# A new order list for the operations of a retention, RWKV and Hyena kernel on one core

## The chip, the cores and the metric

The kernel runs on one core of one Trainium2 chip. The metric is the device time of one execution in microseconds. Engines are named as the profile names them: PE is the matrix engine (PEld its weight loads), DVE the vector engine, ACT the scalar engine, POOL the GpSimd engine, and SP the engine whose queue issues all transfers.

## The reference, cut to what matters

```python
# q, k, v: (2, 8, 768, 64); blocks of 64 tokens
intra = (qb @ kb^T * Dmask) @ vb          # Dmask: powers of lam, lower triangle
inter = (qb * lam_pow) @ kv_state
out_block = intra + inter
kv_state = lam**64 * kv_state + (kb * rev_pow)^T @ vb
# heads joined: x is (2, 768, 512)
xk = mu_k * x + (1 - mu_k) * x_prev;  xr = mu_r * x + (1 - mu_r) * x_prev
y = sigmoid(xr @ w_r) * (relu(xk @ w_k)**2 @ w_v)       # w_k: 512 x 1024, w_v: 1024 x 512
gate = sigmoid(conv5(y, conv_w))                         # five taps over the tokens
result = (gate * (y @ w_val)) @ w_out
```

All weights come as 64-bit floats; everything else is 32-bit.

## The kernel before, in words

**Stages.** There are 1536 tokens, in 12 chunks of 128 (attention), 6 groups of 256, and 3 pairs of groups of 512. A chunk `c` of attention makes transposed k and q, scores, masked scores, a state update and an output; chunks 0 to 3 are done whole, chunks 4 to 11 in halves of 64 tokens. Two groups of attention output give a pair `pr`, on which the layers then run: mix, receptance `r`, hidden `k`, value `v`, gate, val, projection. Each product is done in three passes with a high and a low part of both operands (lines 741 to 757), so an operand must first be split: `h` is a copy in the matrix format on ACT, `l` the remainder on DVE or POOL.

**Weights.** A weight piece is 128 rows of 512 64-bit numbers (512 KB). The function `conversion` (lines 310 to 352) makes 32-bit floats of it by steps named `a`, `b` (ACT, lines 328 and 330), `c`, `d`, `e` (DVE, lines 333 to 339), `f` (DVE or POOL, line 342), and then `h` (ACT, line 346) and `l` (DVE or POOL, line 348). Pieces `w0` to `w3` are w_r, `w4` to `w7` the first half of w_k, `w8` to `w11` its second half, `w12` to `w19` w_v, `y0` to `y3` w_val, `z0` to `z3` w_out.

**The order list.** Nothing is scheduled by the compiler: the string `ORDER` names all 1066 operations in one order, and every engine runs its own operations in that order. `name:E` puts an operation on engine E (V is DVE, G is POOL, A is ACT) where its definition allows more than one. An operation waits for what it reads and for the earlier users of its buffers. The names that matter here:

- `k0`, `q0`, `v0`, `w2`, `lam`, `mu` (a letter or word with one number): a load, issued by SP. The loads of k and q of chunks 0 to 5 are two issues each.
- `jq3.0` to `jq3.3`, `jk3.0` to `jk3.3`: the loads of q and k of group 3 (chunks 6 and 7), four issues of 32 KB each; `Bq3` and `Bk3` transpose them on DVE (line 461).
- `scan`: eight scans on DVE that make the decay mask (line 963); they read `lam` and `eye`. `quar`, `kd0`, `kd1`: copies of it on ACT. `pows`: nine small operations that make the powers `pw` (lines 981 to 998).
- `Tk0`, `Tq0`: four transposes on PE (line 440); `Ek0`, `Eq0`: their way out of PSUM; `Q1`: q times the powers; `D0`: k times its decay (line 480).
- `S0` scores, `M0` mask (lines 501 and 578, DVE), `U0` the state product, `O1` and `N1` the state update (lines 531, 534, 613, 616), `Y4` and `Z0` the output product, `X0` and `H0` its way out.
- `mr0.3.1a`, `b`, `h`, `l`: the mix for r of pair 0, block 3, group 1, and its split (lines 729, 734, 702, 704); `mk0.0a` and so on for k.
- `r0.10.0`: a unit of 12 matmuls of r (line 754); `k0.3.0`, `v0.2.0`, `a0.3.0`: units of 12 of the hidden, value and val products; `p1.0.0`: a unit of 6 wider ones of the projection (line 933).
- `k0.3e`, `h`, `q`, `l`: relu, square and split of the hidden product; `g0.1.2`: a tap of the gate (line 895); `s0.1h`, `l`: the split before val; `p1.0o`: a store.
- `warm3`: four matmuls on the identity without a use of their own.

**Buffers.** The ring `two` has 27 slots of 128x512, the ring `four` 6 of 128x1024, PSUM 4 slots of one bank. A slot is handed out at the first operation that names it, and that operation waits for the users of the slot before. Since SP is one queue, a load that waits for a slot holds all loads behind it.

**POOL and DVE.** In `emit`, every operation on POOL is made to wait for the DVE operation that stands last before it in the list:

```python
if o.engine == "G" and o.port and done is not None and last_v is not None:
    tc.add_manual_dep(done.ins, last_v.name, ..., reason="shared port")
```

Of the kernel before, what the change touches and what calls it, by code (L numbers as in the profile page):

```python
# [18 lines left out]


ORDER = """
    eye warm3 zero table w7 w7a w7c w7d w7e w4 lam w7b w4a w4c w4d w1 w4b w7f:V w4e w0 w1a q0
    Tq0 w4f:V w1c w1d pows k0 warm1 H0 w0a w0c w0d w0e Tk0 w0b k1 q1 warm2 Tk1 w7h Eq0:A k2 mu
    w1b w1e Ek0:A w7l:G w0f:G scan w1f:V S0 w4h w3 kd0 v0 D0:G Ek1:A Tk2 w1h Tq1 muT M0 w1l:V
    Eq1:A w3b w0h Q1 S1 w4l:V q2 D1:G U0 muc N0:A M1 v1 w3a D2:V Z0 X0:A Tq2 Eq2:A w6 Z1 Ek2:A
    w0l:V w3c O1:V Q2 w6a w3d X1:A H1:G q3 U1 w3e w6c mr0.3.0a:A mr0.3.0b mr0.1.0a:A mr0.1.0b
    v2 w6d mr0.0.0a:A mr0.3.0h mr0.3.0l:G S2 Tq3 N1 O2:G mr0.2.0a:A M2 mr0.0.0b k3 Tk3 Eq3:A
    Ek3:A mr0.1.0h w2 q4 Q3 k4 mr0.0.0h mr0.2.0b U2 quar kd1 S3 Z2 Tk4 w2a D3:G mr0.0.0l:G w2b
    M3 N2 X2:A w3f:V mr0.1.0l:V Tq4 v3 O3:V w2c w6b Ek4:A Z3 U3 Eq4:A w6e mr0.2.0h D4:V S4
    X3:A mr0.0.1a:A w2d v4 mr0.3.1a:A mr0.2.0l:G U4 k5 N3 q5 Q4 mr0.0.1b mr0.1.1a:A mr0.1.1b  # L30
# [9 lines left out]
    k0.1.1 w9l:V Q6:V w11h k0.0h w12c k0.3e:A w10e w11l:V k0.0q:A w12d jk5.0 Z5 w10f:V k0.1e:A  # L40
    k0.1h k0.1q:A k0.6.0 k6 D6:G w10h k0.4.0 k0.2e:A k0.2h X5:A M6 w13c w10l:V w16 k0.5.0
    k0.7.0 v10 jq5.2 U6 w13d k0.0l:V w16a N6.0:A w13e H3 w12e w15 w13f:V w15a w15c S7 w12f:V
    Q7:V k0.5.1 Y6 k0.3h O6.1:V w13h w12h w13l:V Z6 w14 N6.1 w15d w15b w12l:V k0.1l:V w14b
    O7.0:V w14a k0.7.1 k0.4.1 k0.7e:A k7 v0.3.0 D7:V X6:A w14c v7 w15e w17a k0.5e:A H2:G w17c
    w15f:G k0.4e:A jq5.1 U7 k0.6.1 N7.0 k0.2q:A k0.4h k0.5h M7 w15h w19 w14d w18 w18a w14e
    w16c w14f:V w17d jq5.3 Y7 w15l:V w16d w14h k0.6e:A k0.3q:A k0.4q:A v0.2.0 k0.2l:V w19a
    k0.3l:V v0.1.0 w14l:V k0.6h w17b w16b w17e k0.5q:A w16e v0.0.0 w17f:V v8 w19c w16f:V w17h
    Z7 w19d w17l:V k11 v0.1.1 w16h jq5.0 k0.7h k0.5l:V w16l:V v0.2.1 k0.4l:V w19e k0.6q:A
    v0.3.1 k0.7q:A k0.6l:V k0.7l:V w19b w19f:V v0.0.1 X7:A jq4.0 mk1.1a:A mk1.0a:A w18c
    mk1.3a:A w18b k9 w19h w18d w18e v0.3.2 w18f:V jk4.3 jq4.2 w18h O7.1:V v0.1.2 w19l:V w18l:V  # L50
    v9 v0.2.2 mk1.2a:A v0.0.2 mk1.1b mk1.1h mk1.0b jk4.1 k8 v0.0.3 mk1.1l:V v0.2.3 jq4.1
# [1033 lines left out]
```

## Time and profile before

| | us |
|---|---|
| median of 3 runs | 304.3 (303.47 to 306.48) |
| the profiled execution | 304.12 |
| its span, first to last instruction | 302.3 |
| PE, DVE, ACT, POOL busy | 279.1, 238.4, 162.6, 64.5 |
| mean granted clock of PE | 0.988 |

The profile shows one execution. Busy time of PE is modelled at the ends of its matmuls, so PE that shows as busy is not always PE at its full rate. L754 is line 754 of the kernel before; in the profile a buffer is named after the operation that first used it, without its first number (`b_mk_0h` is the high part of block 0 of a mix for k).

### The profile page before, as it was taken

The page shows a single profiled execution, that of the slowest core. Times are in us where ns is not written, and L with a number is a line of the kernel's source. Part 1 is how long each engine was busy: PE and PEld are TensorE (multiplying, and loading weights), DVE is VectorE, ACT ScalarE, POOL GpSimd, SP SyncE. Part 2 cuts the span into 40 slices and gives each one's busy share as a digit, 9 for nine tenths or more (in the row PEclk, how much of TensorE's full clock was granted, in tenths as well). Part 3 has the DMA queues.
Part 4 walks back from the last instruction along what each step waited for, and adds up shares of the span by engine and source line. Part 5 has one row for each costly group of instructions (what it writes and reads, how often), then busy time and mean ns, then how long its engine had stood idle before and what let it go on. Part 6 is the DMA issues. An engine that isn't in the chain of part 4 may idle for free.

```text
span 302.3 us, 7580 instructions
## 1 busy us (share of the span) xinstructions
PE 279.1 (92%) x3149; PEld 264.4 (87%) x3149; DVE 238.4 (79%) x397; ACT 162.6 (54%) x303; POOL 64.5 (21%) x69
## 2 busy tenths in 40 slices
PE   1469899869999999999999999999999999999995
...
GB/s 165 279 269 240 171 138 220 176 209 219 166 165 90 89 118 134 13 207 82 16 72 74 0 3 0 2 0 2 38 102 0 2 1 3 0 72 0 104 106 139
DMA packets 63489, 29.37 MB, mean 97 GB/s; under 512 B 58306, under 2 KB 58334, under 8 KB 63454
## 3 DMA queue, kind: packets, MB, share of 16 engines
...
q14 instruction: 10, 0.08, 0.1%
...
## 4 chain that ended last, share of the span: by engine, by line
PE 65%; DMA 12%; DVE 11%; SPq 4%; ACT 4%; issue 3%; DVEq 0%; ACTq 0%
PE b_k L754 16%; PE b_v L754 14%; PE b_p L933 11%; PE b_a L754 11%; PE b_r L754 7%; DMA xx<-in_moe_w_k_dram 5%; SPq L232 4%; DMA xx<-in_moe_w_r_dram 3%; PE xx L655 2%; DMA b_jk<-in_k_dram 2%; DMA b_w<-in_moe_w_v_dram 2%; DVE b_scan L963 1%; DVE w_v L348 1%; PE su L571 1%; DVE b_Bk L461 1%
## 5 line engine op out<-in xcount | busy, mean ns | idle before, releaser
L895 DVE SCALAR_TENSOR_TENSOR b_g<-xx,cw,b_g 128x512 f32<-128x512 f32 x48 | 38.7, 814 | 1.9 <-ACT b_g L897 1.1
L754 PE MATMUL b_k<-b_mk_0h,w_rk 128*128 128x256 f32 x96 | 24.8, 283 | 1.0 <-ACT xx L823 1.0
L754 PE MATMUL b_k<-b_mk_2h,w_rk 128*128 128x256 f32 x96 | 25.7, 291 | 0.0
L754 PE MATMUL b_k<-b_mk_3h,w_rk 128*128 128x256 f32 x96 | 24.5, 280 | 0.0
L754 PE MATMUL b_k<-b_mk_1h,w_rk 128*128 128x256 f32 x96 | 24.2, 277 | 0.0
L754 PE MATMUL b_r<-b_mr_0h,w_rk 128*128 128x256 f32 x96 | 20.1, 284 | 0.0
L754 PEld LDWEIGHTS b_k<-b_mk_0h,w_rk 128*128 128x128 f32 x96 | 18.0, 188 | 1.5 <-ACT xx L823 1.2
L754 PEld LDWEIGHTS b_k<-b_mk_2h,w_rk 128*128 128x128 f32 x96 | 18.6, 193 | 0.7 <-DVE w_rk L348 0.2
L754 PEld LDWEIGHTS b_k<-b_mk_3h,w_rk 128*128 128x128 f32 x96 | 18.4, 192 | 0.0
L754 PEld LDWEIGHTS b_k<-b_mk_1h,w_rk 128*128 128x128 f32 x96 | 18.1, 188 | 0.0
L754 PEld LDWEIGHTS b_r<-b_mr_0h,w_rk 128*128 128x128 f32 x96 | 15.9, 188 | 0.3
L754 PE MATMUL b_k<-b_mk_2l,w_rk 128*128 128x256 f32 x48 | 13.6, 283 | 0.0
L754 PE MATMUL b_k<-b_mk_3l,w_rk 128*128 128x256 f32 x48 | 13.4, 280 | 0.0
L754 PE MATMUL b_k<-b_mk_0l,w_rk 128*128 128x256 f32 x48 | 13.3, 277 | 0.0
L754 PE MATMUL b_k<-b_mk_1l,w_rk 128*128 128x256 f32 x48 | 13.3, 277 | 0.0
L754 PE MATMUL b_r<-b_mr_0l,w_rk 128*128 128x256 f32 x48 | 13.3, 277 | 0.0
L440 PE MATMUL b_Tq<-ident,b_q 128*128 128x128 f32 x24 | 4.8, 327 | 8.8 <-DMA b_q<-in_q_dram 8.8
L754 PE MATMUL b_v<-b_k_0h,w_v 128*128 128x256 f32 x48 | 12.3, 281 | 0.0
L754 PE MATMUL b_v<-b_k_2h,w_v 128*128 128x256 f32 x48 | 12.2, 279 | 0.0
L613 POOL TENSOR_TENSOR state<-state,pw 128x256 f32<-128x256 f32 x4 | 2.5, 622 | 45.4 <-DVE state L616 32.7
L754 PE MATMUL b_a<-b_s_3h,w_rk 128*128 128x256 f32 x48 | 12.1, 277 | 0.0
L754 PE MATMUL b_a<-b_s_2h,w_rk 128*128 128x256 f32 x48 | 12.1, 277 | 0.0
...
## 6 DMA issues: line engine op xcount, KB each, us to landing
...
```

The source lines that it names most:

```text
L232: e.dma_start(to, src)
L348: op(f"{key}l", "VG", lambda e: e.tensor_tensor(r(lo()), words(F32, 1), f32(hi()), op=ALU.subtract), reads=[raw, high, hi], writes=[lo])
L440: e.transpose(ps()[:, C * n:C * n + C], src()[:, C * n:C * n + C], ident)
L461: op(f"B{nm}{g}", "V", lambda e, raw=raw, t=t: e.transpose(t(), raw()), reads=[raw], writes=[t])
L571: e.matmul(su[half[j], s, Q * n:Q * n + Q], kt[half[s], n, t], qt[half[s], n, t], start=True, stop=True,)
L613: op(f"O{c}.{j}", "GV", lambda e, a=state_of[new], o=state_of[old]: e.tensor_tensor(a, o, pw[:, :, Q - 1:Q].to_broadcast([P, NPAIR, D]), o ...
L655: last = e.matmul(x[half[b_], j, at, :], w, m, start=spots[i] not in spots[:i], stop=spots[i] not in spots[i + 1:],)
L754: e.matmul(o, r(a), r(b), start=first and n == 0, stop=last and n == len(todo) - 1)
L895: e.scalar_tensor_tensor(t, src, w, t, op0=ALU.mult, op1=ALU.add)
L933: e.matmul(ps(), x, w, start=u == 0 and n == 0, stop=u == 1 and n == 5)
L963: e.tensor_tensor_scan(dmask_t()[:, s, n, :], lam_t()[:, h:h + 1].to_broadcast([P, C]), ident, 0.0, op0=ALU.mult, op1=ALU.add,)
```

## The change

The list `ORDER` is replaced by another one, with the same operations but for one (`warm7` takes the place of `warm1`), and `pows` may be put on DVE as well as on POOL. 103 of the 1066 operations change their engine: 33 go from DVE to POOL, 28 from POOL to DVE, 21 from DVE to ACT, 18 from ACT to DVE, 2 from POOL to ACT and 1 from ACT to POOL. No function is added. The part of the list up to `Bk3`, before and after, and the other line:

```diff
 ORDER = """
-    eye warm3 zero table w7 w7a w7c w7d w7e w4 lam w7b w4a w4c w4d w1 w4b w7f:V w4e w0 w1a q0
-    Tq0 w4f:V w1c w1d pows k0 warm1 H0 w0a w0c w0d w0e Tk0 w0b k1 q1 warm2 Tk1 w7h Eq0:A k2 mu
-    w1b w1e Ek0:A w7l:G w0f:G scan w1f:V S0 w4h w3 kd0 v0 D0:G Ek1:A Tk2 w1h Tq1 muT M0 w1l:V
-    Eq1:A w3b w0h Q1 S1 w4l:V q2 D1:G U0 muc N0:A M1 v1 w3a D2:V Z0 X0:A Tq2 Eq2:A w6 Z1 Ek2:A
-    w0l:V w3c O1:V Q2 w6a w3d X1:A H1:G q3 U1 w3e w6c mr0.3.0a:A mr0.3.0b mr0.1.0a:A mr0.1.0b
-    v2 w6d mr0.0.0a:A mr0.3.0h mr0.3.0l:G S2 Tq3 N1 O2:G mr0.2.0a:A M2 mr0.0.0b k3 Tk3 Eq3:A
-    Ek3:A mr0.1.0h w2 q4 Q3 k4 mr0.0.0h mr0.2.0b U2 quar kd1 S3 Z2 Tk4 w2a D3:G mr0.0.0l:G w2b
-    M3 N2 X2:A w3f:V mr0.1.0l:V Tq4 v3 O3:V w2c w6b Ek4:A Z3 U3 Eq4:A w6e mr0.2.0h D4:V S4
-    X3:A mr0.0.1a:A w2d v4 mr0.3.1a:A mr0.2.0l:G U4 k5 N3 q5 Q4 mr0.0.1b mr0.1.1a:A mr0.1.1b
-    O4.0:G M4 w2e w3h mk0.0a:A mr0.0.1h r0.01.0 Tk5 N4.0 w2f:V Tq5 w5 w5a w3l:V Eq5:A Ek5:A
-    mr0.1.1h jq3.0 v5 w5c w5b mr0.3.1b mr0.0.1l:V mr0.3.1h mr0.1.1l:V r0.00.0 S5 mk0.0b w5d
-    w2h w2l:V Y4 mr0.2.1a:A mr0.2.1b mr0.2.1h Z4 w6f:V r0.11.0 mk0.1a:A w5e mk0.1b mr0.3.1l:V
-    mr0.2.1l:V w5f:V jq3.2 mk0.3a:A mk0.2a:A w8 mk0.0h mk0.0l:V w9 mk0.2b w8a mk0.3b jq3.1
-    mk0.1h mk0.1l:V w11 w5h w5l:V O4.1:G jk3.0 jq3.3 M5 D5:G Bq3 jk3.1 r0.00.1 w11b w10
-    r0.10.0 w9a r0.00s r0.01.1 w8b r0.01s mk0.3h mk0.3l:V r0.11.1 r0.10.1 r0.11s k0.2.0 jk3.3
-    w9c k0.3.0 mk0.2h mk0.2l:V N4.1 r0.10s O5.0:V w6h w8c X4:A Q5 w10b w9d w9b k0.1.0 w6l:V
-    k0.0.0 w8d w11a w11c w9e k0.0.1 w13 k0.0e:A U5 w12 w9f:G jk3.2 w17 Bk3 w13b N5.0 w8e w11d
...
+    eye zero warm7 lam table scan w2 w2a k0 q0 quar Tk0 mu w2b w3 kd0 w3a w1 w2c w2d w2e w2f:V
+    Tq0 Eq0:A Ek0:V S0 D0:V H0 w2h warm2 k2 k1 w3b Tk1 w3c w1a w3d w3e w3f:V w3h kd1 w0 muT
+    w1b q1 pows:G muc w1c w0a w2l:V w1d Tk2 Ek1:A w3l:V w1e warm3 w1f:V v0 q3 D2:G Tq1 U0 M0
+    w1h Eq1:A N0:A Ek2:A w0c w1l:V S1 Tq3 w0d Q1 w0e q2 k3 D1:G M1 Eq3:A v1 w4 Tq2 Z0 Q3 Eq2:A
+    w0b Q2 X0:A S2 w0f:V O1:G Tk3 Ek3:A D3:G w4a U1 q4 w4b Z1 v2 w0h X1:A mr0.3.0a:A w5 M2 N1
+    O2:V mr0.1.0a:A S3 v3 w4c k4 mr0.2.0a:A U2 w4d w4e w0l:G mr0.0.0a:A Tq4 M3 N2 k5 mr0.2.0b
+    q5 mr0.1.0b Eq4:A w5a w4f:V Z2 X2:A mr0.0.0b w4h w5c mr0.3.0b w5d v4 O3:V mr0.3.0h
+    mr0.1.0h w7 w5e Q4 H1:G Z3 mr0.0.0h w4l:V Tk4 mr0.1.0l:V mr0.2.0h mr0.0.0l:V D4:G U3 Tk5
+    Ek4:A X3:A mr0.2.1a:A N3 S4 M4 Tq5 mr0.2.0l:V mr0.3.1a:A mk0.3a:A mr0.3.1b mr0.3.0l:V
+    mr0.1.1a:A mr0.0.1a:A mr0.0.1b mr0.1.1b Ek5:A O4.0:V Eq5:A r0.00.0 mr0.2.1b w6 mk0.1a:A v5
+    U4 N4.0 mk0.1b O4.1:V S5 w5b mr0.3.1h mk0.0a:A w7a w5f:V r0.01.0 D5:G M5 Y4 r0.01.1 mk0.1h
+    N4.1 mk0.0b mr0.2.1h mr0.1.1h mk0.2a:A mr0.3.1l:V cw0 w7c mr0.0.1h mk0.1l:V Z4 mk0.2b w6a
+    w8 mr0.0.1l:V mr0.1.1l:V mk0.0h mk0.3b w7d w8a r0.00.1 mr0.2.1l:V U5 w5h mk0.3h r0.10.0
+    w6c w10 w7b r0.10.1 w5l:V mk0.2h mk0.0l:V Q5 r0.11.0 r0.11.1 w7e r0.01s O5.0:V w6d r0.00s
+    mk0.2l:V w9 w7f:V r0.10s w6b w12 w6e mk0.3l:V w10b k6 k0.3.0 w6f:V w7h w7l:V w9a w12a w9c
+    w8c w11 w13 w12c w8b w9d w8d k0.2.0 r0.11s w11a w6h w6l:V w10a w10c w9e w11c w9b w13b
+    k0.1.0 jq3.3 w8e w13a jk3.1 N5.0 jq3.0 w13c w12b w11d w11b w9f:V jq3.2 jq3.1 k0.0.0 k0.0.1
+    X4:A w8f:V k0.1.1 w11e v6 w8h jk3.2 w10d w8l:V w9h w10e w9l:V w10f:V k0.3.1 k0.3e:A w12d
+    Y5 k0.1e:A Z5 w11f:V w13d w10h w12e w11h w11l:G Bq3 k0.2.1 k0.0e:A k0.3h k0.2e:A w10l:V
+    Q7:V jk3.3 k0.6.0 jk3.0 k0.4.0 w12f:V Q6:V D6:V k0.7.0 X5:A k0.2h w13e w13f:G k0.1h Bk3
...
-    op("pows", "G", powers, reads=[lam_b], writes=[pw_b])
+    op("pows", "GV", powers, reads=[lam_b], writes=[pw_b])
```


## Rows read from the trace of the kernel before

**Rows 1.** The page, parts 1 and 2: busy time; PE in forty slices of the span.

```profile
PE 279.1 (92%) x3149; PEld 264.4 (87%) x3149; DVE 238.4 (79%) x397; ACT 162.6 (54%) x303; POOL 64.5 (21%) x69
...
PE   1469899869999999999999999999999999999995
```

**Rows 2.** Windows: stretch, us, busy PE PEld DVE ACT POOL (instructions), PE clock, DMA, GB/s.

```profile
5.40:19.20 13.80, 6.55 (x45) 5.69 (x45) 12.75 (x24) 7.01 (x14) 6.91 (x12) 1.00 1.08 252
...
19.20:52.20 33.00, 30.19 (x505) 27.47 (x506) 31.99 (x60) 27.07 (x58) 7.54 (x9) 0.95 0.85 203
...
52.20:66.00 13.80, 10.16 (x94) 9.38 (x92) 9.13 (x18) 10.94 (x20) 2.93 (x3) 1.00 0.79 206
...
66.00:110.00 44.00, 43.06 (x600) 41.39 (x601) 40.70 (x77) 32.58 (x58) 2.65 (x4) 0.96 0.60 142
...
150.00:233.00 83.00, 82.92 (x811) 82.47 (x810) 71.12 (x111) 39.27 (x74) 25.65 (x19) 1.00 0.09 27
```

**Rows 3.** The chain that ended last, in order of time: start, us, what.

```profile
178.62 21.76 PE b_k L754 x192
...
254.79 11.01 PE b_p L933 x48
```

**Rows 4.** Timeline of the start, all engines: start, us, engine, line, operation, [idle before].

```profile
1.63 0.42 SPq L953 DMA_DIRECT2D b_lam<-in_lam_dram  x1
...
4.73 0.66 ACT L328 ACTIVATE b_w7a<-b_w 128x512 f32<-128x512 f32 x1 [2.51 <-DMA b_w<-in_moe_w_k_dram]
...
8.06 0.87 POOL L988 COPY pw<-b_lam 64x4 f32<-64x4 f32 x2 [6.29 <-DMA b_lam<-in_lam_dram]
...
11.34 1.29 PE L440 MATMUL b_Tq<-ident,b_q 128*128 128x128 f32 x4 [8.76 <-DMA b_q<-in_q_dram]
...
13.95 4.74 DVE L963 TENSOR_TENSOR_SCAN b_scan<-b_lam,ident 128x128 f32<-128x128 f32 x8
...
20.69 1.16 PE L494 MATMUL su<-b_Eq,b_Ek 64*128 64x128 f32 x16 [2.81 <-ACT b_Eq L443]
```

**Rows 5.** Timeline of DVE (first five) and PE from 51 to 107 us.

```profile
51.56 0.68 DVE L348 TENSOR_TENSOR w_rk<-xx,w_rk 128x512 fp32r<-128x512 f32 x1
...
53.92 1.25 DVE L461 STREAM_TRANSPOSE b_Bq<-b_jq 128x1024 f32<-128x1024 f32 x1 [1.08 <-DMA b_jq<-in_q_dram]
...
60.99 0.43 DVE L333 TENSOR_SCALAR b_w11a<-b_w11a 128x512 f32<-128x512 f32 x1 [0.94 <-ACT b_w11a L328]
...
64.46 1.25 DVE L461 STREAM_TRANSPOSE b_Bk<-b_jk 128x1024 f32<-128x1024 f32 x1 [2.45 <-DMA b_jk<-in_k_dram]
...
104.91 1.29 DVE L348 TENSOR_TENSOR w_v<-b_w,w_v 128x512 fp32r<-128x512 f32 x2
...
53.80 0.39 PE L754 MATMUL b_k<-b_mk_0h,w_rk 128*128 128x256 f32 x1 [1.00 <-ACT xx L823]
...
106.45 0.28 PE L754 MATMUL b_v<-b_k_6h,w_v 128*128 128x256 f32 x1
```

**Rows 6.** Groups of DVE instructions from 5 to 110 us: busy us, mean ns, idle before.

```profile
L348 DVE TENSOR_TENSOR w_rk<-xx,w_rk 128x512 fp32r<-128x512 f32 x8 | 5.5, 692 | 0.0
...
L704 DVE TENSOR_TENSOR b_mr_0l<-b_mr_0a,b_mr_0h 128x256 fp32r<-128x256 f32 x5 | 1.9, 416 | 0.0
```

**Rows 7.** Timeline of the SP queue: loads of the transposed blocks, four issues each.

```profile
37.92 4.93 SPq L232 DMA_DIRECT2D b_jq<-in_q_dram  x4
...
43.88 2.09 SPq L232 DMA_DIRECT2D b_jq<-in_q_dram  x4
...
50.19 2.16 SPq L232 DMA_DIRECT2D b_jq<-in_q_dram  x4
```

**Rows 8.** Timeline of DVE and of POOL beside each other, late in the span.

```profile
206.29 0.75 DVE L895 SCALAR_TENSOR_TENSOR b_g<-xx,cw,b_g 128x512 f32<-128x512 f32 x1
...
208.63 3.24 DVE L895 SCALAR_TENSOR_TENSOR b_g<-xx,cw,b_g 128x512 f32<-128x512 f32 x3
...
208.88 1.65 POOL L882 TENSOR_TENSOR b_s_3l<-xx,b_s_3h 128x512 fp32r<-128x512 f32 x1 [5.39 <-DVE b_z2a L339]
```

More of the change, by code (lines that the diff above doesn't have):

```diff
@@ L40 @@
[L40 to L51, printed above, removed]
@@ new lines @@
+    O7.0:G M7 Z6 w13h w13l:V w15c w14 k7 k0.6e:A v7 v0.2.0 k0.2q:A w14a k0.2l:V w15b w14c w17a
+    w15d v0.1.0 D7:V w15e w14d U7 k0.7e:A v0.3.0 w15f:V k0.5h w17c k0.5q:A w14e w14b X6:A w15h
+    N7.0 Y7 Z7 w14f:V w16 w14h w16a w15l:V w17d w14l:V jq4.0 w19 k0.7h w16c w17e w17b w18 w16d
+    H3 w17f:V w16e w19a w19c jq4.2 w16b v0.0.0 jk4.2 w16f:V w17h H2:G w18a w17l:V v0.0.1 x0
+    w16h w18c v0.3.1 k0.5l:V w16l:V X7:A k0.4l:V k0.6h w19b w18b w19d w18d w19e k9 w18e w19f:V
+    v9 w18f:V k0.6q:A v0.2.1 mk1.1a:A jq5.1 jk4.0 mk1.3a:A mk1.0a:A k0.6l:V w19h k0.7q:A
@@ new lines @@
+    w19l:V mk1.2a:A v0.1.1 v0.2.2 k0.7l:V w18h w18l:V k8 v0.3.2 mk1.3b jq4.1 v0.1.2 mk1.3h
+    mk1.0b v0.0.2 mk1.1b v0.2.3 mk1.0h mk1.1h mk1.0l:V v0.3.3 v0.3e mr1.3a:A v0.1.3 mk1.2b
+    mk1.1l:V v0.0.3 jq4.3 jk4.1 O7.1:G v0.2e v0.1e k1.1.0 k1.2.0 cw mk1.3l:G N7.1 D9:G v8
+    jk4.3 k1.5.0 Bq4 jq5.3 cwa v0.0e D8:V k1.7.0 mk1.2h jq5.2 mk1.2l:V Q8:V k1.5.1 Bk4 U8 S8
+    x1.1:A k1.2.1 O8.0:G N8.0 M8 Y8 mr1.0a:A k1.1.1 k10 D10:V cwc O8.1:V mr1.2a:A k1.5e:V v10
+    Z8 k1.1e:A N8.1 S9 cwb cwd cwe cwf:G cwg U9 X8:V mr1.0b O9.0:V y2 k1.1h k1.4.0 k1.4.1
@@ new lines @@
+    r1.3.0 k1.7h k1.4l:G k1.0q:A r1.1.1 r1.1s r1.3.1 k1.6h k1.0l:V k1.2q:V k1.2l:V M11 z3a y2d
+    z3c y2e x1.0:A k1.6q:V v1.3.0 x2.3:A k1.7q:A Z11 g0.0.0:A g0.1.2 v1.1.0 r1.0s v1.1.1
+    v1.2.0 v1.2.1 z3d y3b H5:G z3e k1.5h k1.5q:G k1.6l:V y3a x3 z1a X11:A y1 mk2.0a:A z1c
+    k1.5l:G z3f:V mr2.2a:A mk2.2a:V r1.3s mk2.3a:A x2.2:A v1.0.0 mk2.3b v1.2.2 mk2.1a:A y0
+    mk2.1b k1.7l:V mr2.2b mk2.0b mk2.0h y0a mk2.0l:V mk2.1h g0.1.3 z1b v1.3.1 v1.3.2 v1.3.3
+    v1.3e v1.0.1 v1.0.2 y3c y3d y3e y3f:G y1a y1c v1.1.2 y1d v1.1.3 mk2.1l:G v1.0.3 v1.0e
```

81 lines of the change are left out of this document (36 added, 45 removed).

## The prediction

> **What bounds the kernel now.** I read the page first, then the windows, then the chain. PE is busy for 92% of the span, and its forty slices show where it isn't: the first quarter [rows 1]. The windows say who holds it there. From 5.4 to 52.2 us DVE is busy for 12.75 of 13.8 us and 31.99 of 33.0; from 66 to 110 us for 40.70 of 44; while PE has 82.92 of 83 us between 150 and 233 [rows 2]. The later part of the chain is units of PE alone: 16 units of 12 matmuls in 21.76 us, 1.36 us each, and 48 projection matmuls in 11.01 us [rows 3]. So until about 106 us PE gets its operands just as DVE finishes them, and from there on PE runs through.
>
> The hinge is piece `w18`. Its low part is the second of two DVE instructions that end at 104.91 + 1.29 = 106.20 us, and the first value unit that reads it starts at 106.45 [rows 5]. Both lists place the same PE work ahead of that unit: 37 units of r, hidden and value (37 x 1.36 = 50.3 us) and the same transposes, attention products and warm-ups (by PE's groups 29.2 us), 79.5 us in all; so PE is 27 us late there. The same work follows it in both. Hence the end moves as the end of `w18l` on DVE moves, as long as nothing behind it binds.
>
> I count DVE as *work* (each listed operation by its group's mean, less 0.08 us by which neighbours overlap) and *lag* (time minus work). Before, the list up to `w18l` has 160 DVE operations, 87.3 us of work: the lag is 106.2 - 87.3 = 18.9 us. Its parts: 5.4 until DVE starts, since the first piece arrives for ACT at 4.73 [rows 4]; 2.2 more by the end of mask `M0` at 20.4; 2.2 more by the end of `w5l` at 52.24 (42.4 us of work, lag 9.8); 4.5 of waits for late transfers, namely 1.08 for `jq3`, 0.94 for `w11` by way of ACT, 2.45 for `jk3` [rows 5]; 0.6 more by 66 us; and 4.0 from there to 106, of which 2.8 are waits for PE and for ACT behind it. The idle time in the windows is 5.4 + 1.05 + 1.0 + 4.7 + 3.3 = 15.4 [rows 2]; the other 3.5 is instructions that took longer than their mean.
>
> **The change part by part.**
>
> *Amount of work.* Total arithmetic stays. Up to `w18l` the new list has 164 DVE operations, 89.2 us: +1.9. It gives DVE three more half splits (3 x 0.34) and two more `f` steps (2 x 0.61), one `l` step less (-0.61) and two small shifts around the copies of k (+0.3); prices are 692 and 416 ns less the overlap [rows 6]. Over the whole list DVE falls from 217.3 to 215.2, so behind `w18l` it has less than before. ACT rises by 1.7 of 151 and POOL by 3.5 of 63; neither is near full in any stretch [rows 2].
>
> *The start.* Before, `lam` is issued at 1.63, behind two weight pieces, and read at 8.06; the eight scans start at 13.95, after three pieces' work, and the first q arrives at 11.34 [rows 4]. In the new list `lam` is the first issue (at 0.74) and `scan` the first DVE work. The trace shows no `lam` load alone. From below: the last `jq3` load is issued until 52.35 [rows 7] and read at 53.92 [rows 5], 1.6 us later, so 0.74 + 0.42 + 1.6 = 2.8; from above: its own 8.06 - 1.63 = 6.4 us, 7.1. A full 512 KB piece takes 4.0 (0.74 to 4.73), and `lam` is a few KB, so I take 2.9, and scan from 3.3 to 8.0. The masks' copies on ACT then hold `w2b` and so `w2f`, which I put at 0.7 of DVE idle. Lag 4.0 after the start in place of 7.6 at `M0` (3.6 saved), up to 8.2 if `lam` takes its 6.4 (nothing saved). With q0 and k0 as third and fourth large loads, at 250 KB per us [rows 2], q0 is there at about 7 us and not at 11.3; `M0` ends at 13.9 us of work + 4.0 = 17.9, and v0, due at 17, is in time.
>
> *The powers.* `pows` may go to DVE, but the new list keeps it on POOL, later (behind `w3f`). The nine operations take 4.8 us there, from 8.06 on [rows 4]; `Q1` needs them at 18.9 and they end about 18.1. Cost 0, with 1.6 if POOL is held up; gain 0.
>
> *The middle.* Between 20 and 52 us both lists feed DVE with the same kinds of operations, and loads are as dense: I keep the 2.2 lost there before (bounds 0 and 4.4). At 39.4 us of work the r unit `r0.10.0` gets its last split: 39.4 + 4.0 + 2.2 = 45.6, with 29.7 of PE work ahead of it; the first hidden unit comes 5.4 later, at 51.0, against 53.80 [rows 5].
>
> *The j loads.* `Bq3` comes at 60.8 us of DVE work and `Bk3` at 65.6, where `w5l` plus little stood before: at lag 6.2 they are due at 67.0 and 71.8. SP is one queue. In it `k6` waits for a slot of the ring `two` that block 0's split gives back at about 48.6, and `w11`, `w13`, `v6` and eight j loads stand behind it: 48.6 + 1.8 for the single loads + 8 x 2.09 [rows 7] = 67.1, landed 2 later at 69.1. `Bk3` starts near 70.6, so 1.4 hides it, and the three waits of 4.5 us in all go. Without that cover, see the rival.
>
> *To `w18l`.* Of 4.0 lost before from 66 on I keep 2.3: PE's waits shrink as the list puts fewer of DVE's inputs right behind PE (bounds 1.2 and 4.0). Sum: lag 4.0 + 2.2 + 2.3 = 8.5; `w18l` ends at 89.2 + 8.5 = 97.7, which is 8.5 before 106.2. DVE's lag falls by 10.4, and 1.9 goes back as added work.
>
> *Behind it.* PE has 189.5 us of work left and took 298.7 - 106.4 = 192.3; I keep these 2.8 (among them the half-clock stretches that pull the mean to 0.96 [rows 2]), and the 3.6 us from the last matmul to the span's end and 1.8 outside it. The profiled execution took 304.12, 0.2 under the median of 304.3, so the two stand for each other: 304.1 - 8.5 = 295.6.
>
> **The rivals.**
>
> *DVE loses nothing after the start (B).* Lag 4.0 at `w18l`: 93.2, 13.0 earlier, 291.1 us. For it: the list is made from these durations, and 31.99 of 33.0 shows that DVE can be fed. Against: even there 2.2 were lost, and PE would have to be as regular.
>
> *POOL beside DVE (C).* A POOL operation of 1.65 us ran beside three taps on DVE, and these took 3.24 us for 3 x 0.75 = 2.25: 0.99 lost [rows 8]. Eleven POOL operations of 0.6 to 1.4 us stand before `w18l` in the new list; at 0.99 each they cost 10.9 in place of the 4.5 that I keep: 304.1 - 8.5 + 6.4 = 302.0. Against it: before, 13 such operations stood there, and all lengthening was 3.5, under 0.3 each.
> [...]
>
> *The SP queue (D, slower).* Eight j loads stand close behind `k6`. One took 4.93 us where others took 2.09 [rows 7]. If all go at 4.93, they end at 50.4 + 39.4 = 89.8, landed 91.8; `Bk3` ends at 93.1, and the 23.6 us of DVE work from there give `w18l` at 116.7: 304.1 + 10.5 = 314.6. It decides from 3.6 us per load on (then `w18l` is back at 106.2); a slot for `k6` that comes 12 us later does the same. Against: of the loads before, one alone was that slow, and they went at 2 us beside more traffic.
>
> *The list gives nothing where it binds (E).* `pows` doesn't move to DVE; if `lam` lands late and the middle loses 4.4, the lag is 14.9 and the time 302.0: no change that can be told.
>
> **How the numbers follow.** Forecast 0.50, B 0.13, C 0.18, D 0.10, E 0.09. What a measurement here can tell from no change is 1%, 3.0 us: faster is below 301.3. The forecast and B lie there whole, and of C and E, centred just above it, somewhat over half; that makes 0.79 faster. 0.12 is the rest of C and E and D's mild end; 0.09 slower is D. The forecast's own range is 290.5 to 300 (`lam` late: +4.2; the middle: 2.2 either way). The range from B's foot to C's upper side, 289.5 to 303.5, leaves D and the edges out.
>
> **What would show it right or wrong.** Right: scan before 4 us; the first q transposes near 7; DVE busy in all of 5 to 100 us; first hidden unit near 51; no wait for `jq` or `jk` in front of the transposes on DVE; `w18l` near 98; PE without gaps behind it, last matmul near 290. Wrong: idle time before `Bk3` that ends with a DMA (D); DVE splits over 1 us beside POOL (C); scan not before 7 (E); or gaps of PE after 110 us, since then the step "nothing behind it binds" fails.

## The result, and the profile after

| | before | after |
|---|---|---|
| median, us | 304.39 (4 runs) | 294.75 (294.27 to 295.52, 4 runs) |
| ratio to before, 95% interval | | 0.9649 (0.9611 to 0.9686) |
| the profiled execution, us | 304.12 | 294.27 |
| its span, us | 302.3 | 292.5 |
| last matmul ends, us | 298.72 | 288.87 |
| PE, DVE, ACT, POOL busy, us | 279.1, 238.4, 162.6, 64.5 | 278.7, 231.2, 163.7, 75.6 |
| mean granted clock of PE | 0.988 | 1.000 |

The forecast was 295.6 us. The page of the new kernel, parts 1 and 2 (busy time; PE and its clock in forty slices), against [rows 1]:

```profile
PE 278.7 (95%) x3149; PEld 262.6 (90%) x3149; DVE 231.2 (79%) x389; ACT 163.7 (56%) x307; POOL 75.6 (26%) x73
...
PE   3799989999999999999999999999999999999995
...
PEclk9999999999999999999999999999999999999999
```

PE's busy time is the same to 0.4 us; what went is its idle time in the first quarter. The same stretches as in [rows 2], with the same columns:

```profile
5.40:19.20 13.80, 11.17 (x80) 8.95 (x81) 12.86 (x24) 10.48 (x23) 6.03 (x11) 1.00 1.25 274
19.20:52.20 33.00, 30.55 (x503) 26.94 (x502) 32.82 (x66) 28.57 (x56) 7.70 (x8) 1.00 0.84 230
52.20:66.00 13.80, 13.69 (x174) 13.36 (x173) 12.01 (x26) 11.55 (x22) 1.31 (x1) 1.00 0.53 99
66.00:110.00 44.00, 43.55 (x585) 42.03 (x586) 40.54 (x69) 30.94 (x55) 13.89 (x10) 1.00 0.66 155
...
150.00:233.00 83.00, 83.00 (x734) 83.00 (x734) 68.94 (x101) 39.28 (x76) 22.25 (x16) 1.00 0.04 14
```

Read the column of matmuls: from 5.4 to 19.2 us PE is busy for 11.17 us where it was 6.55, and from 52.2 to 66 for 13.69 where it was 10.16. DVE, third of the busy columns, is busy for 32.82 of 33.0 in the second stretch. The clock is 1.00 throughout, where it was 0.95 and 0.96. The timeline of the start, against [rows 4]:

```profile
0.74 0.36 SPq L953 DMA_DIRECT2D b_lam<-in_lam_dram  x1
...
3.70 2.63 DVE L963 TENSOR_TENSOR_SCAN b_scan<-b_lam,ident 128x128 f32<-128x128 f32 x8 [3.70 <-DMA b_lam<-in_lam_dram]
...
7.34 1.21 PE L440 MATMUL b_Tq<-ident,b_q 128*128 128x128 f32 x4
...
10.33 2.08 PE L494 MATMUL su<-b_Eq,b_Ek 64*128 64x128 f32 x16 [1.78 <-ACT b_Eq L443]
```

`lam` is there at 3.70, the first q transposes run at 7.34 and not at 11.34, the first scores at 10.33 and not at 15.54, as the row of before below has it (the row of [rows 4] at 20.69 is `S1`). The eight scans take 2.63 us where they took 4.74.

```profile
15.54 1.16 PE L494 MATMUL su<-b_Eq,b_Ek 64*128 64x128 f32 x16
```

The timeline of DVE around the j loads and at the end of `w18l`, against [rows 5]:

```profile
65.53 1.25 DVE L461 STREAM_TRANSPOSE b_Bq<-b_jq 128x1024 f32<-128x1024 f32 x1 [1.33 <-issue]
...
70.90 1.25 DVE L461 STREAM_TRANSPOSE b_Bk<-b_jk 128x1024 f32<-128x1024 f32 x1 [0.55 <-DMA b_jk<-in_k_dram]
...
95.86 0.69 DVE L348 TENSOR_TENSOR w_v<-b_w,w_v 128x512 fp32r<-128x512 f32 x1
```

and the SP queue in front of them, against [rows 7]: `k6`, which waited for its slot, then the j loads.

```profile
47.25 0.38 SPq L232 DMA_DIRECT2D b_k<-in_k_dram  x1
...
48.78 1.91 SPq L232 DMA_DIRECT2D b_jq<-in_q_dram  x4
50.73 4.69 SPq L232 DMA_DIRECT2D b_jk<-in_k_dram  x4
...
55.46 6.14 SPq L232 DMA_DIRECT2D b_jq<-in_q_dram  x12
...
62.15 7.36 SPq L232 DMA_DIRECT2D b_jk<-in_k_dram  x12
```

The last j load is issued until 69.51 (67.1 was worked out), one of the eight loads at 4.69 us and the others at 1.9 to 2.5. `Bk3` starts at 70.90 (70.6) and waits 0.55 us instead of 2.45: the cover was 0.5 us too thin, no more. In front of `Bq3` the page names no cause; the last of `jq3`'s issues, at 61.16, took 4.1 us to land (median of those beside it 2.0), so this 1.33 too was most likely a load's. `w18l` ends at 95.86 + 0.69 = 96.55, 9.65 earlier than the 106.20 of [rows 5]; the last matmul comes 9.85 earlier.

### The profile page after: what moved, and what is told of

Same layout as the page of the kernel before. It is cut to its first block, busy times and chain, and to the rows that moved or that the text cites. A ratio compares the mean times of both kernels' runs of the same rounds, so it can differ in the third digit from the quotient of the medians.

```text
span 292.5 us, 7610 instructions
## 1 busy us (share of the span) xinstructions
PE 278.7 (95%) x3149; PEld 262.6 (90%) x3149; DVE 231.2 (79%) x389; ACT 163.7 (56%) x307; POOL 75.6 (26%) x73
## 4 chain that ended last, share of the span: by engine, by line
PE 84%; DVE 5%; ACT 4%; SPq 2%; DMA 2%; issue 1%; DVEq 0%; ACTq 0%
PE b_v L754 23%; PE b_k L754 19%; PE b_p L933 11%; PE b_r L754 11%; PE b_a L754 11%; PE xx L655 3%; SPq L232 2%; PE xx L553 2%; DMA xx<-in_moe_w_v_dram 1%; PE su L571 1%; PE su L592 1%; DMA b_lam<-in_lam_dram 1%; DVE b_scan L963 1%; DVE b_M L501 1%; PE su L494 1%
## 5 line engine op out<-in xcount | busy, mean ns | idle before, releaser
L895 DVE SCALAR_TENSOR_TENSOR b_g<-xx,cw,b_g 128x512 f32<-128x512 f32 x48 | 44.7, 952 | 0.5
L754 PE MATMUL b_k<-b_mk_2h,w_rk 128*128 128x256 f32 x96 | 24.9, 283 | 0.0
L754 PEld LDWEIGHTS b_k<-b_mk_2h,w_rk 128*128 128x128 f32 x96 | 18.0, 188 | 0.4
L903 ACT ACTIVATE b_g<-b_g 128x512 f32<-128x512 f32 x12 | 7.3, 628 | 15.6 <-DVE b_g L895 15.6
L870 DVE TENSOR_TENSOR xx<-b_v,xx 128x512 f32<-128x512 f32 x12 | 8.1, 683 | 6.9 <-PE b_v L754 6.8
L754 PE MATMUL b_v<-b_k_1h,w_v 128*128 128x256 f32 x48 | 12.2, 279 | 0.2 <-ACT b_k_7e L847 0.2
L754 PE MATMUL b_a<-b_s_1h,w_rk 128*128 128x256 f32 x48 | 12.1, 276 | 0.0
```

Source lines behind the costliest of these rows:

```text
L754: e.matmul(o, r(a), r(b), start=first and n == 0, stop=last and n == len(todo) - 1)
L870: op(f"v{pr}.{rb}e", "V", lambda e: e.tensor_tensor(x2_at(pr, rb), two(ps), x2_at(pr, rb), op=ALU.mult), reads=[ps], writes=[x2_b[pr, rb]])
L895: e.scalar_tensor_tensor(t, src, w, t, op0=ALU.mult, op1=ALU.add)
L903: op(f"g{pr}.{n}s", "A", lambda e: e.activation(acc(), acc(), AF.Sigmoid), writes=[acc])
```

## Where the time went

DVE's account up to `w18l`, from the traces of the two kernels. An instruction's time counts from the end of the one before it, and what it takes beyond its group's mean is lengthening. The scans turned out to take 2.63 us when nothing holds them; they count 2.63 in the work of both:

| us up to the end of `w18l` | before | after |
|---|---|---|
| DVE starts | 5.4 | 3.7 |
| idle afterwards | 10.0 | 4.1 |
| instructions longer than their mean | 5.6 | 1.6 |
| work | 85.2 | 87.1 |
| end | 106.2 | 96.5 |

So 1.7 us came from the start, 5.9 from waits, 4.0 from instructions that no longer grow, and 1.9 went into more work. Of the 4.0 some 3.3 stand in instructions that overlap one on POOL. This is DVE's account, not a price list: some of its parts, put alone into the old list, gain nothing, as the experiments show.

PE's account says what reached the end. Busy time up to the first unit that reads `w18`, before and after, with the columns of [rows 2]:

```profile
0.00:106.45 106.45, 87.63 (x1214) 81.31 (x1214) 91.07 (x168) 78.16 (x148) 21.20 (x35) 0.97 0.76 185
...
0.00:97.38 97.38, 87.56 (x1214) 79.71 (x1214) 89.56 (x173) 78.47 (x148) 26.54 (x33) 1.00 0.80 197
```

The same 1214 matmuls take the same 87.6 us; PE's idle time falls from 18.8 to 9.8 us. Of these 9.0 us, 3.3 fall before 20 us, 1.5 between 20 and 38, and 4.2 behind. From 39 us on PE waits in the new list for nothing longer than 0.23 us.

## The experiments

Line numbers of the experiments' kernels are 5 lower than those above, since the list takes fewer lines. First the parts of the gain, put one by one into the list of before.

**The start alone.**

```diff
-    eye warm3 zero table w7 w7a w7c w7d w7e w4 lam w7b
+    eye warm3 zero table lam scan w7 w7a w7c w7d w7e w4 w7b
...
-    w1b w1e Ek0:A w7l:G w0f:G scan w1f:V
+    w1b w1e Ek0:A w7l:G w0f:G w1f:V
```

> The list of before, with lam issued first and the scans first on DVE; nothing else moves. Theory (the gain is a sum of DVE's lag saved at the start and of waits for transfers taken away later): DVE is about 4 us earlier until 50 us, but Bq3 and Bk3 still wait for loads that SP issues at its own pace, so most of it goes into a longer wait in front of Bk3 (2.45 us before, 4 to 6 now): 302.5 to 304.4. Rival (the start alone explains nearly half of the change): 300.0 to 300.8, with Bk3's wait near 2.5.

Measured: 304.62 us, ratio 0.9976 (0.9937 to 1.0016). The timeline of DVE, where it waits:

```profile
3.46 2.85 DVE L958 TENSOR_TENSOR_SCAN b_scan<-b_lam,ident 128x128 f32<-128x128 f32 x8 [3.46 <-DMA b_lam<-in_lam_dram]
...
17.28 1.22 DVE L496 TENSOR_TENSOR b_M<-su,b_scan 128x1024 f32<-128x1024 f32 x1 [2.22 <-PE su L489]
...
63.28 1.25 DVE L456 STREAM_TRANSPOSE b_Bk<-b_jk 128x1024 f32<-128x1024 f32 x1 [3.56 <-DMA b_v<-in_v_dram]
```

The scans are done 12 us earlier, but the mask needs scores, and these need q, which still lands at 11.4: 2.22 us are lost there. `Bk3` takes another 3.56. `w18l` ends at 105.98, 0.2 earlier than before. An early `lam` alone is worth nothing in the old list. The rival falls; the theory holds in its direction only: DVE is 1.9 us earlier at the first mask (18.50, not 20.41), not 4, the wait in front of `Bk3` is under its 4 to 6, and the time lies 0.2 above its range.

**One transpose out of the way.** `Bk3` behind five other DVE operations, and its reader `S6` two units later:

```diff
-    U5 w12 w9f:G jk3.2 w17 Bk3 w13b N5.0 w8e w11d
-    w8f:V w11e w13a w12a k0.2.1 w10a w10c Y5 S6 w9h k0.3.1
+    U5 w12 w9f:G jk3.2 w17 w13b N5.0 w8e w11d
+    w8f:V w11e Bk3 w13a w12a k0.2.1 w10a w10c Y5 w9h k0.3.1
...
-    w11f:V w12b k0.1.1 w9l:V
+    w11f:V w12b k0.1.1 S6 w9l:V
```

> The list of before, with Bk3 moved five DVE operations later (behind w11e) and S6, which reads it, two units later on PE. Theory: DVE works through its 2.45 us wait for jk3, PE's 3.0 us wait for the state in front of S6 goes: DVE 2.0 to 2.5 earlier from there on, 301.8 to 302.5. Rival (the wait is hidden anyway, since the next splits wait for something else): 303.8 to 304.6.

Measured: 301.27 us, ratio 0.9888 (0.9841 to 0.9934). In DVE's timeline the wait is gone:

```profile
64.55 1.25 DVE L456 STREAM_TRANSPOSE b_Bk<-b_jk 128x1024 f32<-128x1024 f32 x1
```

`w18l` ends at 103.12, 3.1 earlier, and the time is 3.5 us under the runs beside it: more than the 2.45 of the wait and a little more than the theory gave. Two more waits of the kernel before are gone here, PE's in front of `Y5`, for the state that `N5.0` makes behind `Bk3`, and a later one of DVE for PE:

```profile
66.16 0.69 PE L655 MATMUL xx<-b_Q,state 64*64 64x64 f32 x16 [2.78 <-DVE state L616]
...
88.31 0.42 DVE L616 TENSOR_TENSOR state<-su,state 128x256 f32<-128x256 f32 x1 [1.23 <-PE su L592]
```

In this execution the wait for `jq3` is 0.9 us shorter too, which the edit doesn't explain, and DVE's instructions are 1.7 us longer, so the parts are not to be taken to the tenth. Two names moved give a third of the whole gain.

**Both.**

> Both edits together on the list of before. Theory: more than the sum, since the early start is no longer lost in front of Bk3: 4 to 6 us, 298.5 to 300.5. Rival (each is hidden by something else in turn): 302 or more.

Measured: 301.21 us, ratio 0.9890 (0.9843 to 0.9936): no more than with `Bk3` alone. The theory falls; the time lies 0.8 under the rival's 302, but its mechanism, that something else hides the early start, is what the timelines show. PE's and DVE's:

```profile
28.45 0.84 PE L435 MATMUL b_Tk<-ident,b_k 128*128 128x128 f32 x4 [2.21 <-DMA b_k<-in_k_dram]
```

```profile
32.06 1.23 DVE L496 TENSOR_TENSOR b_M<-su,b_scan 128x1024 f32<-128x1024 f32 x1 [1.71 <-PE su L489]
```

The old list asks for `k3` so late that PE waits 2.21 us for it, and the mask `M3` on DVE 1.71 for PE. In the new list the loads of k and q follow the scans forward, so the lead is kept, as the next run shows.

**The start taken out of the new list.** `lam` third:

```diff
-    eye zero warm7 lam table scan w2 w2a k0 q0 quar
+    eye zero warm7 table w2 w2a k0 lam scan q0 quar
```

> The new list with lam issued third, behind w2 and k0, as it stood behind two pieces before. Theory: the scans start at about 8 instead of 3.70, DVE has nothing else in front of them, and its lag is 3.5 to 4.5 larger up to w18l: 298.2 to 299.3. Rival (the start is absorbed by slack later): 294.5 to 295.3.

Measured: 296.61 us, ratio to before 0.9739 (0.9692 to 0.9787). `lam` lands 2.6 us later and not 4:

```profile
6.33 2.63 DVE L958 TENSOR_TENSOR_SCAN b_scan<-b_lam,ident 128x128 f32<-128x128 f32 x8 [6.33 <-DMA b_lam<-in_lam_dram]
```

`w18l` ends 2.1 later and the time is 1.9 longer. Both expectations are missed, the theory's by its size: I had put the landing at 8. What is lost at the start passes on to the end nearly one for one, which in the old list it did not.

**A wait of ACT.** On top of the `Bk3` run, `N6.0` behind `w15a` on ACT:

```diff
-    k0.0l:V w16a N6.0:A w13e
+    k0.0l:V w16a w13e
...
-    w13f:V w15a w15c
+    w13f:V w15a N6.0:A w15c
```

> The list of before with Bk3 and S6 later, as in the run that came to 301.27, and with N6.0 on ACT moved behind w15a, so that ACT's wait for PE no longer stands in front of w15. Theory (what DVE lost between 66 and 106 us were waits for other engines at the heads of queues): the 1.59 us wait of w15c on DVE goes, 299.5 to 300.2. Rival (another wait takes its place before w18): 301.0 to 301.5.

Measured: 305.58 us, ratio 1.0019 (0.9975 to 1.0062): both fall. ACT's timeline in the run that it builds on:

```profile
75.30 0.38 ACT L605 ACTIVATE state<-su 128x256 f32<-128x256 f32 x1
77.56 0.67 ACT L323 ACTIVATE b_w15a<-xx 128x512 f32<-128x512 f32 x1 [1.88 <-DMA xx<-in_moe_w_v_dram]
```

and ACT's and PE's in this one:

```profile
78.50 0.66 ACT L323 ACTIVATE b_w15a<-xx 128x512 f32<-128x512 f32 x1 [2.56 <-DMA xx<-in_moe_w_v_dram]
```

```profile
79.48 0.69 PE L566 MATMUL su<-b_Bq,b_Bk 64*64 64x64 f32 x32 [2.91 <-ACT state L605]
```

In the `Bk3` run `w15a` was held by its own load, not by `N6.0`, which was done 1.9 us before. The premise came from the profile of before, where ACT does run the two back to back, behind a wait of 2.24 us for PE. With `N6.0` moved behind `w15a`, the state update came late for PE. In this execution another 2.62 us of DVE went in front of `Bq3` at 54.53, ahead of the edit, so how much of the 4.3 us to the `Bk3` run the edit cost stays open. A wait that is named after an engine can be a transfer's that this engine waits for, as here the 1.88 us of `w15a`'s load, and it is to be read in the profile of the list that is edited.

**Powers beside the scans, and powers on DVE.** Two runs of the new list, `pows` directly behind `lam`, and `pows:V` at its place:

```diff
-    eye zero warm7 lam table scan w2
+    eye zero warm7 lam pows:G table scan w2
...
-    w1b q1 pows:G muc w1c
+    w1b q1 muc w1c
```

```diff
-    w1b q1 pows:G muc w1c
+    w1b q1 pows:V muc w1c
```

> The new list with pows put directly behind lam, so that POOL makes the powers while DVE runs the eight scans. Theory (a POOL operation beside a DVE operation with two operands lengthens it): the scans take 4.4 to 4.9 us instead of 2.63, DVE is 1 to 2 us later at the first mask, of which the stretch of the old place of pows gives back up to 1: 295.0 to 296.3. Rival (the scans were long before for another reason): scans 2.6 to 2.9, 294.0 to 294.9.

> The new list with the nine operations of pows on DVE at the same place, which the other line of the change permits. Theory: 9 operations of 0.1 to 0.2 us on the engine that is full there, 1 to 1.8 us, less the 0.5 to 1 us by which POOL's powers lengthened DVE between 10 and 16 us: 294.9 to 296.0. [...]

The first took 294.91 us (0.9660, 0.9635 to 0.9685), no different from the new list, and the theory's mechanism fails for operations as small as these: with the powers beside them the scans took 2.85 us, 0.22 more than in the new list:

```profile
3.75 2.85 DVE L958 TENSOR_TENSOR_SCAN b_scan<-b_lam,ident 128x128 f32<-128x128 f32 x8 [3.75 <-DMA b_lam<-in_lam_dram]
```

The second took 296.60 us (0.9719, 0.9687 to 0.9750), 1.85 more than the new list and a little beyond what the theory gave. The nine operations on DVE:

```profile
12.54 0.34 DVE L983 COPY pw<-b_lam 64x4 f32<-64x4 f32 x2
12.92 1.85 DVE L989 TENSOR_TENSOR pw<-pw 128x4 f32<-128x4 f32 x7
```

They take 2.2 us, not 1 to 1.8, and the first mask ends 1.6 later (19.21, not 17.61): some 0.6 comes back from DVE's instructions that POOL's powers had lengthened, as the theory had it. Leaving `pows` on POOL was right, and that part of the change changes nothing.

**The choice of engines.** The new order, first with all 103 operations on their old engine, then with only those 20 up to `w18l` that moved between DVE and POOL; of each the first lines that change:

```diff
-    Tq0 Eq0:A Ek0:V S0 D0:V H0 w2h
+    Tq0 Eq0:A Ek0:A S0 D0:G H0 w2h
...
```

```diff
-    Tq0 Eq0:A Ek0:V S0 D0:V H0 w2h
+    Tq0 Eq0:A Ek0:V S0 D0:G H0 w2h
...
-    v0 q3 D2:G Tq1
+    v0 q3 D2:V Tq1
...
```

> The new order with every operation on the engine it had before (103 operations go back; pows stays on POOL in both). DVE has 2.3 us less work up to w18l and POOL some six operations more. Theory (the order carries the gain, and a POOL operation costs DVE about 0.3 us): 293.0 to 295.5. Rival (choosing engines is what gains; about 1 us per POOL operation): 297.5 or more.

> The new order, where only the 20 operations up to w18l that go from DVE to POOL or back are given to the engine they had before. Theory (it is the meeting of POOL operations with DVE operations of the kinds c, d, f and b that costs): most of the 5.9 us which all old engines cost, 298.5 to 300.5, with instructions on DVE up to 0.8 us longer than their mean beside POOL. Rival (the copies that moved between ACT and DVE, or the choices behind w18l, make it): 294.5 to 297.0.

The first took 300.62 us (0.9860, 0.9808 to 0.9912), the second 297.75 us (0.9759, 0.9717 to 0.9801). So, in the new order, 5.9 of the 9.6 us depend on the choice of engines, as the rival of the first had it, and 3.0 on those 20 (the second lies between its two expectations). Up to `w18l` only one more operation differs, the copy `Ek0`; the other 82 choices stand behind it. In the first's profile `w18l` ends at 100.00, 3.4 later than in the new list, and 1.8 us more are lost behind it, so a good part of the rest stands there. The profiled execution of the second, at 299.15 us, was the longest of its four; its `w18l` ends at 101.79. The profile of the second shows how 20 choices cost 3 us although they take 1.7 us of work off DVE. POOL and DVE beside each other, at three places:

```profile
9.84 1.04 POOL L475 TENSOR_TENSOR b_k<-b_k,kdec 128x512 f32<-128x512 f32 x1 [8.06 <-ACT b_w3a L323]
9.87 1.34 DVE L328 TENSOR_SCALAR b_w3a<-b_w3a 128x512 f32<-128x512 f32 x1 [0.17 <-ACT b_w3a L323]
...
25.08 1.05 POOL L475 TENSOR_TENSOR b_k<-b_k,kdec 128x512 f32<-128x512 f32 x1
25.57 0.84 DVE L328 TENSOR_SCALAR b_w4a<-b_w4a 128x512 f32<-128x512 f32 x1
...
73.62 1.43 POOL L475 TENSOR_TENSOR b_k<-b_k,kdec 128x512 f32<-128x512 f32 x1 [8.12 <-DMA xx<-in_moe_w_v_dram]
74.17 1.42 DVE L337 CUSTOM_DVE_ANT_0 xx<-xx,b_w13a 128x1024 uint16<-128x1024 uint16 x1
```

A step `c`, 0.43 us alone [rows 5], took 1.34 and 0.84, a step `f` 1.42 where others take 0.69. Over the list up to `w18l` all lengthening is 6.8 us with 18 POOL operations of over 0.5 us (the powers left out), 5.6 with 15 before, and 1.6 with 13 in the new list, where masks (`M`), state updates (`N`) and transposes stand beside POOL, and none of these grew by over 0.1 us.

**The new engines in the old order.** The list of before with the engines of the new one:

```diff
-    Ek0:A w7l:G w0f:G scan
+    Ek0:V w7l:V w0f:V scan
...
```

> The list of before with every operation on the engine that the new list gives it (103 operations), in the old order. DVE has 1.9 us more work up to w18l. Theory (the choice of engines pays only in the order it was made for, where POOL's operations stand beside masks and state updates; Bk3's wait stays): 303.0 to 306.5. Rival (the choice pays by itself, as it cost 5.9 us to undo it): 298.5 to 301.5.

Measured: 313.69 us, ratio 1.0201 (1.0102 to 1.0301): slower by more than either gave. The theory's direction holds, that the choice pays only in the order it was made for, but not its size. `w18l` ends 2.1 later, about the 1.9 us of added work; 7.0 arise behind it, which no rival had. PE's groups of instructions from 110 us on, with the idle time in front of them and what ended it:

```profile
L749 PE MATMUL b_a<-b_s_2l,w_rk 128*128 128x256 f32 x24 | 6.7, 281 | 1.6 <-POOL b_s_2l L877 1.6
L650 PE MATMUL xx<-b_Q,state 64*64 64x64 f32 x128 | 3.6, 229 | 1.7 <-POOL xx L783 1.3
L587 PE MATMUL su<-b_v,b_k 64*64 64x64 f32 x112 | 2.7, 222 | 1.5 <-POOL b_k L475 1.5
```

For 1.6 + 1.3 + 1.5 = 4.4 us PE waits there for operations on POOL, which come too late for their place. Of the other 2.6, 0.99 is a wait for a mask on DVE; the rest stays open. This run also settles the scans. In it `w7l` and `w0f` are on DVE and nothing on POOL overlaps the scans:

```profile
16.43 2.63 DVE L958 TENSOR_TENSOR_SCAN b_scan<-b_lam,ident 128x128 f32<-128x128 f32 x8
```

In the kernel before, the two stood on POOL, 1.30 and 1.41 us from 14.16 to 16.83, within the scans of 4.74 us [rows 4]. They cost 2.1 of their 2.7 us; the small powers had cost 0.2. Yet neither this run nor the early start alone, where the scans took 2.85, was faster than the kernel before: in the old list those 2 us are lost again elsewhere.

**Can the new list be beaten?** PE's waits in it, behind the start, are few; the longest, 1.26 us, stands in front of `S5`:

```profile
37.92 0.69 PE L571 MATMUL su<-b_Eq,b_Ek 64*64 64x64 f32 x32 [1.26 <-ACT xx L330]
```

Six moves fill it:

```diff
-    S5 w5b mr0.3.1h mk0.0a:A w7a w5f:V r0.01.0 D5:G M5
+    w5b mr0.3.1h mk0.0a:A w7a w5f:V r0.01.0 S5 D5:G M5
...
-    w11l:G Bq3 k0.2.1 k0.0e:A k0.3h k0.2e:A w10l:V Q7:V
+    w11l:G w10l:V Bq3 k0.2.1 k0.0e:A k0.3h k0.2e:A Q7:V
...
-    k0.1h Bk3 k0.1q:A k0.1l:V
+    k0.1h k0.1q:A k0.1l:V Bk3
...
-    S6 k0.0h k0.0q:A k0.0l:V w15 w12h w17 N6.0:A O6.1:G k0.6.1
-    M6 Y6 S7 w15a k0.5e:A w12l:V k0.7.1 N6.1 O7.0:G M7 Z6 w13h w13l:V
+    k0.0h k0.0q:A k0.0l:V w15 w12h w17 N6.0:A O6.1:G k0.6.1 S6
+    M6 Y6 w15a k0.5e:A w12l:V k0.7.1 S7 N6.1 O7.0:G Z6 w13h w13l:V M7
```

> The new list with six moves: S5 behind r0.01.0, S6 behind k0.6.1, S7 behind k0.7.1, M7 behind w13l, w10l in front of Bq3, Bk3 behind k0.1l. Theory (in the new list PE is late by what it waits in the first 43 us, and 1.26 us of that stands in front of S5; behind it PE has no gap, so a gap filled there moves the end if DVE's low parts stay ahead): 293.3 to 294.0, ratio to before 0.962 to 0.965. Rival (DVE sets the pace of the middle in the new list too, so the gap only moves to a later unit): 294.5 to 295.2.

Measured: 294.76 us, ratio to before 0.9649 (0.9612 to 0.9686): the rival's number, the new list's to 0.01, but its mechanism isn't shown. PE was 1.5 us earlier from 44 to 72 us (`r0.10.0` at 43.76, not 45.30), and lost this again in two stops: 1.11 us inside the first value unit, behind a step on DVE that doesn't feed it, and 0.63 us among the matmuls of an output product, which the profile puts down to nothing. `w18l` ended at 96.62 as in the new list (96.55); DVE in its turn waited for `S7`, which the edit had moved back. DVE's wait, and PE's longer stop:

```profile
75.56 0.42 DVE L611 TENSOR_TENSOR state<-su,state 128x256 f32<-128x256 f32 x1 [1.15 <-PE su L566]
```

```profile
78.01 0.38 PE L749 MATMUL b_v<-b_k_0h,w_v 128*128 128x256 f32 x1 [1.11 <-DVE b_w15a L328]
```

**DVE's waits out as well.** On top of the run before:

```diff
-    k0.1l:V Bk3 k0.4.1 k0.5.0 k0.3q:A k0.4e:A k0.4h k0.3l:V
+    k0.1l:V k0.4.1 k0.5.0 k0.3q:A k0.4e:A k0.4h k0.3l:V Bk3
...
-    w12h w17 N6.0:A O6.1:G k0.6.1 S6
-    M6 Y6 w15a k0.5e:A w12l:V k0.7.1 S7 N6.1 O7.0:G Z6
+    w12h w12l:V w17 N6.0:A O6.1:G k0.6.1 S6
+    M6 N6.1 O7.0:G Y6 w15a k0.5e:A k0.7.1 S7 Z6
```

> The new list with the moves of the run before (S5, S6 and S7 later, w10l in front of Bq3) and three more that let DVE work through its own waits: Bk3 behind k0.3l, w12l in front of M6, N6.1 and O7.0 in front of S7. Theory (DVE sets the pace up to w18l in the new list too, so the end moves only with what is taken from DVE's idle time, 0.65 + 0.55 + 1.15 us of it here, as far as PE's own lead of 1.5 us lets it): w18l at 94.3 to 95.3, 293.0 to 293.9. Rival (PE alone sets the pace from 43 us on): 294.5 to 295.2 as in the run before.

Measured: 297.55 us, ratio to before 0.9744 (0.9701 to 0.9786). Of eight executions one took 293.03 us at a granted clock of 1.000; the profiled one took 295.82 at 0.998, and the other six 297.35 to 298.35 at 0.992 to 0.994. The profiled one has `w18l` at 97.28, since instructions on DVE grew by 1.4 us more than in the run before, and PE stands still for 1.95 us in the middle of a value unit, which the profile puts down to nothing. The run also holds a move that the expectation doesn't name: `M5` stands in front of `D5`.

```diff
-    r0.01.0 S5 D5:G M5 Y4
+    r0.01.0 S5 M5 D5:G Y4
```

`D5` on POOL then waits for `M5` and runs beside a mix on DVE, which takes 1.42 us and not 0.87:

```profile
40.08 1.04 POOL L475 TENSOR_TENSOR b_k<-b_k,kdec 128x512 f32<-128x512 f32 x1 [5.15 <-DVE b_M L573]
40.25 1.42 DVE L729 SCALAR_TENSOR_TENSOR b_mk_0a<-b_H,rest,b_mk_0a 128x512 f32<-128x512 f32 x1
```

So the run tests neither theory cleanly, and no version here is shown to beat the new list; the one execution at 293.03 is under all four of it.

**One number over all runs.** Time of the profiled execution less the end of `w18l` on DVE: 197.9 before, 197.7 after, and between 197.4 and 199.5 in eleven of the twelve experiments, while the times went from 294.7 to 306.0. That is what the prediction's hinge said: behind this point PE runs through. The new engines in the old order have 204.9: there it fails, since PE waits behind this point too.

## Why the prediction was right

It was right in its time (295.6 against 294.27 for the profiled execution, whose sum it is) and in most of its steps:

- *The hinge* held in its number: 9.65 us at `w18l`, 9.85 at the last matmul. Its reason no longer holds in the new list: PE reaches the first unit that reads `w18` at 97.38, 0.8 after the split is made, and from 39 us to there nothing stops it for more than 0.23 us. What DVE gained beyond PE's pace is slack, so that the two numbers agree to 0.2 is in part luck. The prediction also counts 37 units ahead of that one and has PE 27 us late; there are 36, and PE was idle for 18.8 us, with 87.6 of busy time and not 79.5. Both lists have the same work there, so the difference stands.
- *Amount of work*, +1.9: the account above has the same; no run contradicts it.
- *The start*: `M0` at 17.61 (17.9 was forecast), lag 3.7 (4.0). That is luck in part: the scans took 2.63 us and not 4.7, but they started at 3.70 and not at 3.3, DVE stood idle for 0.9 and not 0.7, and its instructions up to `M0` took some 1.3 us more than their usual time, half of it beside the powers on POOL.
- *The powers*: nothing waited for them, as forecast; they ended at 15.93, before `Q1` at 18.81. Their cost wasn't 0: the run with `pows:V` has DVE some 0.6 us shorter around them.
- *The middle*: mis-sized. I kept the 2.2 us lost there before; it was 0.6 (`mr0.1.1l` at 43.71 with 39.4 us of work). `r0.10.0` came at 45.30 (45.6), 1.6 after that split, and the first hidden unit at 50.86 (51.0), because PE was late by then: it had waited 1.26 us in front of `S5`. So these two numbers were right for another reason.
- *The j loads*: within 2.4 us over a queue of 20 us. The waits didn't go wholly: 4.5 became 1.9, 0.55 by a load and 1.33 in front of `Bq3`, most likely by one. The sign that the prediction gave for D, idle time before `Bk3` that ends with a DMA, did come, at 0.55 us.
- *To `w18l`*: I kept 2.3 from 50 us on; it was 3.1. Sum of lag 8.5, measured 7.4.
- *Behind it*: I kept 2.8, it was 2.0 (288.87 - 97.38 = 191.5 us for 189.5 of work). The half-clock stretches that the 2.8 counts in lie ahead of `w18`: before, the clock was 0.50 from 22 to 25 us and from 67 to 69, and 1.00 from 106 us to the last matmul.

What the argument did not see is why the lag falls. It gave all 10.4 us of it to the start, the late transfers and PE's shorter waits. The profiles show 4.0 of 11.5 in instructions on DVE that no longer grow, most of them beside POOL. The sum carried this lengthening along, 2.1 us of it as the price of the scans and the rest among the losses that it keeps; it was itself a thing that the new choice of engines, in its own order, removes. And it took the start for a saving by itself; in the old list the start alone gave nothing, and `Bk3` with it nothing more than `Bk3` alone, while in the new list the start is worth 1.9.

Rival C, POOL beside DVE, was right in its mechanism and wrong in its sign for this list: it is what the old choice costs in the new order (3.0 to 5.9 us), and what the new choice avoids. Its 0.99 for each operation is no common price: the scans lost 2.1 us beside two POOL operations of 2.7 us together, and a step `c` grew by 0.9 beside one of 1.04, but masks and state updates `N`, one input of which lies in PSUM, grew beside POOL by at most 0.1. What makes the difference no run shows. Rival D didn't come: one j load in eight went at 4.69, not all. Rival B, with no loss after the start, had the middle nearly right (0.6), but not the 3.1 behind it. Of E, that `pows` doesn't go to DVE holds, and costs nothing.
